# Attention and routed experts on one core: 512-column idle products, the fp16 identity made on GpSimd, and a new hand-written issue order

## The chip, the cores and the metric

One core of one Trainium2 chip. The time is that of the device, in microseconds (us), for one execution of the whole program; less is better. Engines: PE is TensorE (products), PEld its weight loads, DVE is VectorE, ACT ScalarE, POOL GpSimd, SP the engine that issues most transfers. Each engine takes its own instructions in order.

## What is computed

```python
# attention, per batch and head
q_s = exp(q - max(q, -1));  q_s /= sum(q_s, -1) + 1e-9
k_s = exp(k - max(k, seq)); k_s /= sum(k_s, seq) + 1e-9
kv  = einsum('bhsd,bhse->bhde', k_s, v)
x   = einsum('bhsd,bhde->bhse', q_s, kv)      # -> rows of 512, B*S = 8*576 rows
# routing, row after row within a batch
fresh_e = argmax(x @ w_gate)                   # 8 experts
e = fresh_e if s == 0 or sigmoid(x @ w_local) < 0.5 else prev_e
out = softmax(x @ w_gate)[e] * (relu(x @ w1[e]) @ w2[e])   # 512 -> 1024 -> 512
```

## The kernel before

The 4608 rows are four tiles t of 1152 (two batches each). Rows of one expert are gathered into blocks of 128. The first nine blocks, all of one expert, are drawn from tiles 0 and 1 alone, so that their products can run while tiles 2 and 3 are still in attention; after them come the blocks of the other experts, some 29 more.

The work up to block 8 is some 770 named tasks. Each has an engine, and `SWAP` lists the tasks that go to their second choice of engine. `ORDER` is one long list of the names; `emit` walks it and each engine gets its tasks in that sequence. No scheduler changes it afterwards. Names that matter here (a number behind a name is the batch, tile or block):

- `Lk Lv Lq`: loads of k, v, q (SP). `max kT kr ka kc sub exp`: the column maximum of k (DVE), its turn on PE, its spread (PE), a copy (ACT), the subtraction (DVE or POOL) and the exponential (ACT). `vc`: a copy of v. `mul`: the product of k and v, two halves a batch, 144 PE instructions each. `nsum norm turn hi lo KW put`: its normalization, and the gate's share of it.
- `qm qs qT qe`: the same for q. `xm xc inv xs ex gs`: a row group's product, its copy, and its store, and the gate's logits of a group.
- `g.* g1 .. g4 ra rp rb ac ab`: the routing of a pair of tiles, a chain of small DVE operations with short PE products between; `ro` makes one of 18 one-hot matrices (DVE, or two operations on ACT); `am` is the product that finds each block's rows; `ax` their indices.
- `G Gp`: gathers of a block's rows and shares (POOL); `Px Ph Pl` scale them and split them into two fp16 parts; `T`/`Tc` or `D` turn them; `W Wh Wl`: load and split of the first expert's weights; `F1 F2`: the block's two products, in halves of 96 and 24 instructions; `Ar Al` the ReLU and its fp16 rest; `Gv Pt`: scale the result (ACT) and scatter it (POOL).
- `RN.9`: ACT (high part) and DVE (rest) overwrite w1 with the second expert's; `s1 s2` load it in fp32. Block 9's code is written behind the list.
- `I`: an idle task, products of the identity that nobody reads:

```python
    def idle_mul(_):
        for i in range(8):
            nc.tensor.matmul(pd[:, 0:P], id16, id16, start=True, stop=True)
```

The `y` result has two buffers, so `Gv` of block 8 waits until the scatter `Pt` of block 6 has landed. The two turned maxima of k (`pz`) share one tile: an operation that reads one half waits for the last writer ahead of it in the list.

Of the kernel before, what the change touches and what calls it, by code (L numbers as in the profile page):

```python
# [116 lines left out]
Lk.0.0 I.72 Lk.0.1 max.0.0 max.0.1 kT.0 Lk.1.0 max.1.0 c2.1 Lq.0.0 Lk.1.1 kr.0 I.8 Lv.0.0 qm.0.0 ka.0 Lk.2.0 Lv.0.1 Lk.2.1 max.1.1 kc.0 qs.0.0 Lk.3.0  # L117
sub.0.0 vc.0.0 qs.0.1 exp.0.0 I.79 I.83 sub.0.1 qT.0.0 I.4 max.2.0 kT.1 I.15 kr.1 max.2.1 c2.0 qe.0.0 I.54 qT.0.1 ka.1 Lv.1.0 Lv.1.1 mul.0.0 vc.0.1
exp.0.1 qs.0.2 kc.1 vc.1.0 mul.0.1 max.3.0 I.78 qe.0.1 kT.2 sub.1.0 I.44 exp.1.0 Lk.3.1 cs sub.1.1 I.18 nsum.0 kr.2 I.20 ka.2 norm.0 Lk.4.0 vc.1.1
exp.1.1 I.13 Lv.2.0 qT.0.2 I.28 kc.2 Lv.2.1 max.3.1 Lq.0.1 mul.1.0 c2.2 mul.1.1 sub.2.1 sub.2.0 turn.0 qe.0.2 kT.3 vc.2.0 max.4.0 I.35 hi.0 kr.3  # L120
nsum.1 exp.2.0 Lk.4.1 I.29 norm.1 lo.0 exp.2.1 vc.2.1 ka.3 turn.1 mul.2.0 mul.2.1 Lk.5.0 sub.3.0 kc.3 hi.1 lo.1 qm.0.1 sub.3.1 exp.3.0 Lv.3.0 KW.0
nsum.2 norm.2 max.4.1 KW.1 put.0 put.1 xm.0.0 xm.0.1 xc.0.0 xc.0.1 qs.0.3 qs.0.4 qT.0.3 Lv.3.1 turn.2 qe.0.3 hi.2 qs.0.5 xm.0.2 qT.0.4 xc.0.2 qm.0.2
qe.0.4 xm.0.3 vc.3.0 lo.2 kT.4 xc.0.3 vc.3.1 kr.4 inv.0.0 Lk.5.1 xm.0.4 mul.3.0 exp.3.1 mul.3.1 KW.2 max.5.0 Lq.1.0 xc.0.4 Lv.4.0 qT.0.5 put.2 qs.0.6
nsum.3 qT.0.6 xs.0.0 norm.3 qe.0.5 qs.0.7 xm.0.5 qe.0.6 ex.0.0 qT.0.7 ka.4 xc.0.5 qe.0.7 max.5.1 turn.3 hi.3 inv.0.1 xm.0.6 qs.0.8 xc.0.6 qm.1.0
qs.1.0 lo.3 qT.0.8 gs.0.0 qm.1.1 ex.0.1 qe.0.8 kT.5 qm.1.2 qs.1.1 xm.0.7 KW.3 Lq.2.0 qs.1.2 qT.1.0 vc.4.0 put.3 xc.0.7 gs.0.1 qT.1.1 kr.5 qe.1.0
qe.1.1 kc.4 qs.1.3 xm.0.8 qT.1.2 xc.0.8 qe.1.2 xm.1.0 qT.1.3 xm.1.1 xc.1.0 qe.1.3 qs.1.4 xc.1.1 inv.0.2 qs.1.5 Lk.6.0 sub.4.0 xm.1.2 ex.0.2 xs.0.1
qT.1.4 qe.1.4 ka.5 xc.1.2 qT.1.5 exp.4.0 qs.1.6 qm.2.0 inv.1.0 xm.1.3 xm.1.4 gs.0.2 max.6.0 qe.1.5 qs.1.7 xc.1.3 xc.1.4 qT.1.6 qe.1.6 qT.1.7 qe.1.7
xm.1.5 sub.5.0 xc.1.5 qs.1.8 xs.0.2 ex.1.0 xm.1.6 qT.1.8 inv.1.1 xc.1.6 xm.1.7 qe.1.8 xc.1.7 xm.1.8 Lv.4.1 Lq.2.1 kc.5 I.21 qs.2.0 sub.4.1 xc.1.8
ex.1.1 Lv.5.0 gs.1.1 gs.1.0 exp.4.1 inv.1.2 mul.4.0 Lv.5.1 qT.2.0 ex.1.2 vc.4.1 qm.2.1 vc.5.0 gs.1.2 qe.2.0 mul.4.1 Lk.6.1 I.45 g.0.p0 qs.2.1 exp.5.0
g.0.p1 g.0 qT.2.1 nsum.4 Lv.6.0 g1.0 xs.1.2 qe.2.1 norm.4 g2.0 turn.4 mul.5.0 sub.5.1 g3.0 Lv.6.1 max.6.1 kT.6 g4.0 hi.4 vc.5.1 ra.0 I.1 exp.5.1 rp.0  # L130
vc.6.0 xs.1.1 lo.4 kr.6 I.24 vc.6.1 rb.0.p0 rb.0 ka.6 kc.6 Lk.7.0 mul.5.1 ro.0.4 Lk.7.1 ac.p0 nsum.5 I.43 I.68 W.0 ro.0.5 sub.6.0 ac ab norm.5 I.25
ro.1.7 ro.0.1 ro.0.3 I.39 ro.1.6 Lv.7.0 ro.1.2 W.1 qs.2.2 ro.1.0 I.53 KW.4 turn.5 ro.1.1 I.88 exp.6.0 ro.0.6 I.36 ro.1.5 ro.0.7 xs.1.0 ro.0.0 qs.2.3
ro.1.3 oe hi.5 Lq.2.2 mul.6.0 Wh.0 sub.6.1 exp.6.1 ro.0.2 put.4 I.48 mul.6.1 lo.5 max.7.0 Wl.0 ro.1.8 qs.2.4 KW.5 ro.0.8 I.33 nsum.6 ro.1.4 put.5
norm.6 qT.2.2 qe.2.2 am I.87 max.7.1 ax.p0 vc.7.0 xm.2.0 xc.2.0 Lv.7.1 kT.7 Wh.1 xm.2.1 ax.p1 xc.2.1 ax kr.7 W.2 G.0 ka.7 qT.2.3 kc.7 xm.2.2 qm.2.2
qT.2.4 sub.7.0 qs.2.5 qe.2.3 I.2 xc.2.2 sub.7.1 turn.6 qs.2.6 Wl.1 exp.7.0 Px.0 vc.7.1 of mul.7.0 inv.2.0 exp.7.1 mul.7.1 Lq.3.0 hi.6 qe.2.4 Ph.0 G.1
W.3 W.4 Wh.2 lo.6 nsum.7 KW.6 norm.7 qT.2.5 xs.2.0 xm.2.3 Pl.0 qs.2.7 put.6 T.0 qe.2.5 qT.2.6 Wl.2 xc.2.3 qm.3.0 Tc.0 Wh.3 xm.2.4 Wh.4 G.2 Sa.0 Px.1
F1.0.0 W.5 qe.2.6 Sb.0 Ar.0.0 turn.7 G.3 xc.2.4 Ph.1 Wl.3 hi.7 G.4 Wl.4 Al.0.0 Wh.5 qs.2.8 lo.7 Pl.1 F1.0.1 KW.7 Wl.5 Ar.0.1 qT.2.7 qs.3.0 W.6 qs.3.1
# [1112 lines left out]
```

## Time and profile before

| | us |
|---|---|
| median of 3 runs (lowest, highest) | 567.36 (566.24, 568.11) |
| the profiled execution, its own time | 568.54 |
| its span, first to last instruction | 566.8 |
| PE busy (share of the span) | 506.1 (89%) |
| DVE, ACT, POOL busy | 284.4, 221.1, 245.1 |
| profiled instructions | 18611 |

1.7 us of the profiled execution lie around the span. From about 128 us on PE is nearly always busy, so there what counts is PE's work and its few gaps; ahead of that PE mostly waits for others.

### The profile page before, as it was taken

The numbers are of one execution on the slowest core, as the hardware profiler recorded it, in microseconds if no ns is written. First come the engines' busy times: TensorE is split into PE (matmuls) and PEld (weight loads), VectorE is DVE, ScalarE is ACT, GpSimd is POOL, SyncE is SP. The second block draws the span as 40 slices with busy tenths as digits, with TensorE's granted clock in tenths as the row PEclk, the third lists the DMA queues.
The fourth block names the chain that finished last, engine by engine and source line by source line (L and its number), as shares of the span: only waits on it lengthen the run. The fifth ranks groups of instructions, "written<-read, shape, count | busy, mean of one in ns | idle before, by whom it ended". The sixth has DMA issues, their size and how long they took to land. (4 is left out here: it accounts for less than half of the span.)

```text
span 566.8 us, 18611 instructions
## 1 busy us (share of the span) xinstructions
PE 506.1 (89%) x7538; PEld 377.1 (67%) x7538; DVE 284.4 (50%) x487; ACT 221.1 (39%) x382; POOL 245.1 (43%) x260
## 2 busy tenths in 40 slices
...
GB/s 313 376 303 270 184 248 337 225 273 296 222 162 84 144 82 157 244 166 117 243 73 112 221 230 90 131 281 122 62 245 216 93 98 62 93 88 63 97 86 52
DMA packets 81541, 98.63 MB, mean 174 GB/s; under 512 B 46719, under 2 KB 56959, under 8 KB 81408
## 3 DMA queue, kind: packets, MB, share of 16 engines
...
q8 instruction: 83, 1.36, 1.1%
...
## 5 line engine op out<-in xcount | busy, mean ns | idle before, releaser
L900 PE MATMUL ph<-xT,w1h 128*128 128x128 f16 (+1 forms) x2432 | 180.3, 218 | 0.0
L900 PEld LDWEIGHTS <-w1h 128*128 128x128 f16 x2432 | 144.8, 98 | 0.0
L903 PE MATMUL ph<-xT,w1l 128*128 128x128 f16 (+1 forms) x1216 | 115.8, 218 | 9.2 <-DVEq L984 6.8
L912 DVE SCALAR_TENSOR_TENSOR lo<-ph,hi 128x512 f16<-128x512 f32 x76 | 52.3, 688 | 129.8 <-ACTq L984 114.2
L930 POOL DMA_INDIRECT out<-y,sidx x38 | 39.1, 1029 | 176.6 <-ACTq L984 140.8
L908 ACT ACTIVATE hi<-ph 128x512 f16<-128x512 f32 x76 | 45.2, 595 | 167.9 <-PE ph L900 115.4
L903 PEld LDWEIGHTS <-w1l 128*128 128x128 f16 x1216 | 82.0, 98 | 25.8 <-DVEq L984 7.0
L923 PEld LDWEIGHTS <-hi 128*128 128x128 f16 x608 | 56.3, 98 | 54.8 <-issue 1.1
L923 PE MATMUL py<-w2h,lo 128*128 128x512 f16 x184 | 69.8, 379 | 1.9 <-DVE lo L912 1.9
L923 PE MATMUL py<-w2h,hi 128*128 128x512 f16 x184 | 69.8, 379 | 0.0
L923 PE MATMUL py<-w2l,hi 128*128 128x512 f16 x184 | 69.7, 379 | 0.0
L863 DVE SCALAR_TENSOR_TENSOR x<-xn,x 128x512 f16<-128x512 f32 x37 | 30.1, 814 | 69.1 <-ACT x L188 65.1
L840 POOL DMA_INDIRECT xg<-xrows,gidx x42 | 47.1, 1122 | 35.0 <-DVE gidx L715 16.7
L923 PEld LDWEIGHTS <-lo 128*128 128x128 f16 x304 | 29.8, 98 | 38.9 <-DVE lo L912 2.9
L846 POOL DMA_INDIRECT pb<-shares,gidx x39 | 40.9, 1050 | 15.0 <-issue 6.0
L923 PE MATMUL pi<-w2h,hi 128*128 128x512 f16 x120 | 46.1, 384 | 0.0
L923 PE MATMUL pi<-w2l,hi 128*128 128x512 f16 x120 | 46.0, 383 | 0.0
L923 PE MATMUL pi<-w2h,lo 128*128 128x512 f16 x120 | 46.0, 383 | 0.0
L851 POOL TENSOR_TENSOR xn<-xg 128x512 f32<-128x512 f32 x34 | 36.3, 1068 | 11.6 <-DMA xg<-xrows,gidx 9.4
L926 ACT ACTIVATE y<-py,pb 128x512 f32<-128x512 f32 x23 | 15.8, 688 | 43.2 <-PE py L923 26.5
L350 PE MATMUL pd<-id 128*128 128x128 f16 x240 | 19.8, 240 | 11.4 <-DVE id L166 11.1
L353 DVE TENSOR_REDUCE KM<-KT 128x128 f32<-128x1152 f32 x13 | 28.2, 2182 | 3.5 <-DMA KT<-in_k 3.5
...
## 6 DMA issues: line engine op xcount, KB each, us to landing
...
```

The source lines that it names most:

```text
L350: nc.tensor.matmul(pd[:, 0:P], id16, id16, start=True, stop=True)
L353: nc.vector.tensor_reduce(out=KM[b % 2][:, 2 * u:2 * u + 2], in_=of(home("k", b, u), b, u).rearrange("p g c d -> p g d c"), axis=AX.X, op= ...
L840: nc.gpsimd.indirect_dma_start(out=xg[b % AHEAD], out_offset=None, in_=src, in_offset=bass.IndirectOffsetOnAxis(ap=i_[:, j_:j_ + 1], axis=0))
L846: nc.gpsimd.indirect_dma_start(out=pb[b % NPB], out_offset=None, in_=src, in_offset=bass.IndirectOffsetOnAxis(ap=i_[:, j_:j_ + 1], axis=0))
L851: eng.tensor_tensor(out=xn[b % 2].rearrange("p (g x d) -> p g x d", g=4, x=2), in0=xg[b % AHEAD].rearrange("p (g x) -> p g x", g=4)[:, :, ...
L863: nc.vector.scalar_tensor_tensor(out=x2[b % 2][:, 1, :], in0=xn[b % 2], scalar=XS, in1=x2[b % 2][:, 0, :], op0=ALU.mult, op1=ALU.subtract)
L900: nc.tensor.matmul(ph_[:, f, 0:n], W["w1h"][:, c, fs], xT_[:, i, c, 0:n], start=False, stop=(c == 3 and i == 1))
L903: nc.tensor.matmul(ph_[:, f, 0:n], W["w1l"][:, c, fs], xT_[:, 0, c, 0:n], start=(c == 0), stop=False)
L908: nc.scalar.activation(hi[b % 2][:, 4 * g:4 * g + 4, :], phs[g], AF.Relu)
L912: nc.vector.scalar_tensor_tensor(out=lo[b % 2][:, gs_, :], in0=phs[g], scalar=0.0, in1=hi[b % 2][:, gs_, :], op0=ALU.max, op1=ALU.subtract)
L923: nc.tensor.matmul(result(b), h_[:, f, :], w_[:, f, :], start=(f == 0 and i == 0), stop=(f == 7 and i == 2))
L930: nc.gpsimd.indirect_dma_start(out=outr, out_offset=bass.IndirectOffsetOnAxis(ap=i_[:, j_:j_ + 1], axis=0), in_=ys[b % 2], in_offset=None, ...
```

## The change

Three edits. An idle task issues two products of 512 columns in place of eight of 128 (four PE instructions for sixteen). The fp16 identity is cast by POOL, not DVE. `SWAP` and `ORDER` are replaced; there are 29 idle tasks where there were 30. All line numbers behind the tables grow by one.

```diff
 SWAP = """
-vc.0.0 norm.0 put.0 vc.1.1 put.1 vc.2.1 put.2 vc.3.0 vc.3.1 put.3 sub.4.1 norm.4 put.4 norm.5 put.5 norm.6 put.6 vc.7.0 vc.7.1 sub.7.1 put.7 gs.0.0
...
+vc.1.1 norm.1 put.1 vc.2.0 vc.2.1 norm.2 put.2 vc.3.0 vc.3.1 put.3 sub.4.1 norm.4 put.4 norm.5 put.5 vc.6.1 put.6 vc.7.0 vc.7.1 sub.7.1 norm.7 ex.0.0
...
 ORDER = """
-Lk.0.0 I.72 Lk.0.1 max.0.0 max.0.1 kT.0 Lk.1.0 max.1.0 c2.1 Lq.0.0 Lk.1.1 kr.0 I.8 Lv.0.0 qm.0.0 ka.0 Lk.2.0 Lv.0.1 Lk.2.1 max.1.1 kc.0 qs.0.0 Lk.3.0
...
+Lk.0.0 Lk.0.1 Lv.0.0 Lk.1.0 max.0.0 Lk.1.1 max.0.1 c2.1 I.65 kT.0 max.1.0 Lq.0.0 kr.0 ka.0 Lv.0.1 max.1.1 kc.0 qm.0.0 Lk.2.0 vc.0.0 Lv.1.0 c2.0
...
     id16 = cp.tile([P, P], F16, name="id16")
-    nc.vector.tensor_copy(out=id16, in_=ident)
+    nc.gpsimd.tensor_copy(out=id16, in_=ident)
...
     def idle_mul(_):
-        for i in range(8):
-            nc.tensor.matmul(pd[:, 0:P], id16, id16, start=True, stop=True)
+        for i in range(2):
+            nc.tensor.matmul(pd, id16, id16.unsqueeze(1).to_broadcast([P, 4, P]), start=True, stop=True)
```

**First place: PE, the first k-v products.** Before, `mul.0` (the two rows of 36) stands behind seven idle tasks and is followed by another; `pz` rows are `kT` and `ka`.

```order
L470 MATMUL pq<-ident,qs 128x128 x4
L368 MATMUL pz<-ident,mt 64x128 x4
L403 MATMUL pa<-VP_123,KT_115 64x65 x36
L403 MATMUL pa<-VP_124,KT_116 64x65 x36
L350 LDWEIGHTS id_67
L350 MATMUL pd<-id_67 128x128
```

After, on PE at the same place:

```order
L404 MATMUL pa<-VP_123,KT_115 64x65 x36
L404 MATMUL pa<-VP_124,KT_116 64x65 x36
L359 MATMUL pz<-ident,KM_126 128x128 x2
L369 MATMUL pz<-ident,mt 64x128 x4
L432 MATMUL pq<-ident,R_134 128x128 x2
L404 MATMUL pa<-VP_125,KT_117 64x65 x36
L471 MATMUL pq<-ident,qs 128x128 x4
```

Three idle tasks of four instructions stand ahead of these, and none between `mul.0` and `mul.1` (the third row of 36).

**Second place: DVE, the routing of tiles 0 and 1.** Before, from `g2` (the scan into `cs`) to `rb` (the first `pf` with `pq`); the row into `KM` is `max.6.1`.

```order
L572 SCALAR_TENSOR_TENSOR cs<-pq,va 1x256
L353 TENSOR_REDUCE KM_126<-KT_115 128x128
L583 TENSOR_TENSOR E<-pq,nA 128x18
L584 TENSOR_TENSOR E<-E,sc 128x18
L586 TENSOR_TENSOR OH<-E,iota_em 128x72 x2
L619 SCALAR_TENSOR_TENSOR pf<-cj,OH 128x144
L621 CAST cc<-pf 128x16
L438 SCALAR_TENSOR_TENSOR kvT<-pq,kvT 128x256
L362 TENSOR_REDUCE mt<-pz 128x4
L633 TENSOR_TENSOR pf<-pf,pq 128x144
```

After, on DVE:

```order
L573 SCALAR_TENSOR_TENSOR cs<-pq,va 1x256
L584 TENSOR_TENSOR E<-pq,nA 128x18
L585 TENSOR_TENSOR E<-E,sc 128x18
L587 TENSOR_TENSOR OH<-E,iota_em 128x72 x2
L620 SCALAR_TENSOR_TENSOR pf<-cj,OH 128x144
L622 CAST cc<-pf 128x16
L354 TENSOR_REDUCE KM_126<-KT_115 128x128
L634 TENSOR_TENSOR pf<-pf,pq 128x144
```

`max.6.1` has moved behind `ra`, where DVE waits for PE's `rp` anyway, and `lo.4` and `kr.6` have left the chain.

**Third place: the hand-over to the second expert, on DVE and POOL.** Before, DVE from `RN.9.0` (w1l) to `RN.9.1`; the row into `x` is `Pl.9`, the rows into `cB` and `info` the last piece of `bj`, the row into `lo` is `Al.8.0`.

```order
L946 SCALAR_TENSOR_TENSOR w1l<-s_3429,w1h 128x4x128 x4
L984 UNCONDITIONAL_BRANCH x2
L863 SCALAR_TENSOR_TENSOR x_1842<-xn_1840,x_1842 128x512
L789 TENSOR_REDUCE cB<-g2B 1x43
L790 TENSOR_TENSOR info_78<-cB,erB 1x43
L791 TENSOR_SCALAR info_78<-wB 1x43
L792 CAST info_78<-wB 1x43
L912 SCALAR_TENSOR_TENSOR lo_1853<-ph_2147,hi_1851 128x512
L984 COMPARE_AND_BRANCH
L946 SCALAR_TENSOR_TENSOR w1l<-s_3429,w1h 128x4x128 x4
```

After, on DVE (the row into `xn` is `Px.11`):

```order
L947 SCALAR_TENSOR_TENSOR w1l<-s_2915,w1h 128x4x128 x4
L985 UNCONDITIONAL_BRANCH x2
L852 TENSOR_TENSOR xn_1719<-xg_1717 128x512
L718 TENSOR_SCALAR tz_3839<-tk_3838 128x43
L719 SCALAR_TENSOR_TENSOR sidx_77<-tk_3838,tz_3839 128x43
L985 COMPARE_AND_BRANCH
L947 SCALAR_TENSOR_TENSOR w1l<-s_2915,w1h 128x4x128 x4
L985 UNCONDITIONAL_BRANCH x2
L913 SCALAR_TENSOR_TENSOR lo_1732<-ph_1981,hi_1730 128x512
```

`Al.8.0`, for which PE's `F2.8.0` waits, now stands behind `RN.9.1`; `bj` has left this stretch. On POOL before, from `Pt.5` to `Pt.6` (the rows into `out` are `Pt.5`, `Pt.7`, `Pt.6`; the row into `xg` is `G.12`, and `L860`/`L861` are `Pl.11`):

```order
L930 DMA out<-y_1856,sidx_73 4608x512
L984 UNCONDITIONAL_BRANCH
L930 DMA out<-y_1856,sidx_73 4608x512
L846 DMA pb_1848<-shares,gidx_76 128x1
L851 TENSOR_TENSOR xn_1840<-xg_1838 128x512
L984 UNCONDITIONAL_BRANCH
L860 TENSOR_SCALAR xn_1840<-xn_1840 128x512
L861 TENSOR_TENSOR x_1842<-xn_1840,x_1842 128x512
L840 DMA xg_1835<-xrows,gidx_76 128x592
L886 UNCONDITIONAL_BRANCH
L930 DMA out<-y_1855,sidx_73 4608x512
```

After, on POOL (`Pt.5`, `Px.10`, `G.12`, `Pt.6`, then `Pt.7` and `Pl.11`):

```order
L931 DMA out<-y_1735,sidx_73 4608x512
L852 TENSOR_TENSOR xn_1718<-xg_1716 128x512
L841 DMA xg_1714<-xrows,gidx_76 128x592
L931 DMA out<-y_1734,sidx_73 4608x512
L985 UNCONDITIONAL_BRANCH
L931 DMA out<-y_1735,sidx_73 4608x512
L985 UNCONDITIONAL_BRANCH
L861 TENSOR_SCALAR xn_1719<-xn_1719 128x512
L862 TENSOR_TENSOR x_1721<-xn_1719,x_1721 128x512
```

`Pt.6` now stands ahead of `Pt.7` and `Pl.11`. Elsewhere: `F1.0.0` now has 14 `mul`, 23 `qT` and 22 `xm` ahead of it on PE, where it had 16, 25 and 23; the same work stands behind it.

## Rows read from the trace of the kernel before

**Rows 1.** Busy time (count) by engine in the hand-over; granted clock, DMA share, GB/s

```profile
core 0: us, PE busy (x) PEld busy (x) DVE busy (x) ACT busy (x) POOL busy (x), PEclk, DMA share, GB/s
241.40:274.50 33.10, 22.25 (x204) 14.69 (x202) 17.20 (x27) 8.85 (x17) 15.52 (x14) 0.90 0.69 147
```

**Rows 2.** The page's DMA queues: packets, MB, share of 16 engines

```profile
q8 instruction: 83, 1.36, 1.1%
```

**Rows 3.** The same windows view, cut where PE stood still twice

```profile
0.00:27.05 27.05, 9.93 (x222) 8.59 (x223) 18.82 (x21) 7.31 (x10) 13.97 (x37) 1.00 0.97 343
27.05:45.08 18.03, 13.16 (x381) 11.84 (x381) 12.23 (x15) 8.82 (x15) 10.09 (x11) 0.89 0.93 322
```

**Rows 4.** PE in order of time: start, us, what [idle before <-releaser]

```profile
27.06 0.34 PE L403 MATMUL pa<-VP,KT 64*64 64x65 f32 x6 [3.62 <-issue]
...
33.10 2.33 PE L403 MATMUL pa<-VP,KT 64*64 64x65 f32 x144
...
45.09 0.48 PE L403 MATMUL pa<-VP,KX 64*64 64x65 f32 x5 [4.32 <-issue]
```

**Rows 5.** DVE in order of time, early

```profile
28.76 1.36 DVE L384 TENSOR_TENSOR KT<-KT,pz 128x1152 f32<-128x1152 f32 x1 [3.97 <-PE pz L358]
```

**Rows 6.** DVE in order of time, first and second routing

```profile
82.51 1.70 DVE L456 TENSOR_REDUCE qm<-qt 128x24 f32<-128x1536 f32 x1
...
84.92 2.06 DVE L543 SCALAR_TENSOR_TENSOR fl<-L,st 128x18 f32<-128x18 f32 x1
...
97.79 2.53 DVE L639 TENSOR_SCALAR lb<-lb 128x18 f32<-128x18 f32 x1
...
195.59 0.40 DVE L543 SCALAR_TENSOR_TENSOR fl<-L,st 128x18 f32<-128x18 f32 x1
...
209.01 0.28 DVE L639 TENSOR_SCALAR lb<-lb 128x18 f32<-128x18 f32 x1
```

**Rows 7.** POOL in order of time, first routing

```profile
84.30 2.63 POOL L384 TENSOR_TENSOR KT<-KT,kb 128x1152 f32<-128x1152 f32 x1
...
97.66 2.63 POOL L384 TENSOR_TENSOR KT<-KT,kb 128x1152 f32<-128x1152 f32 x1 [8.62 <-ACT kb L378]
```

**Rows 8.** ACT in order of time, the first of the one-hot matrices

```profile
100.56 0.40 ACT L650 ACTIVATE da<-iot,off 128x128 f32<-128x128 f16 x1 [2.98 <-DVE off L640]
101.00 0.49 ACT L651 ACTIVATE oo<-da,val,nval 128x128 f16<-128x128 f32 x1
```

**Rows 9.** PE in order of time: `am`, and the start of `F1.0.0`

```profile
112.06 0.60 PE L704 MATMUL pq<-oba,oo 128*128 128x9 f16 x18 [1.13 <-ACT R L188]
...
127.89 0.38 PE L903 MATMUL ph<-xT,w1l 128*128 128x128 f16 x4
```

**Rows 10.** PE in order of time: one `xm`, one `qT`

```profile
66.19 0.75 PE L483 MATMUL pa<-R,qe 64*64 64x74 f32 x32
...
67.17 0.65 PE L470 MATMUL pq<-ident,qs 128*128 128x128 f32 x4
```

**Rows 11.** PE in order of time: five idle tasks; a 512-column product

```profile
99.60 2.41 PE L350 MATMUL pd<-id 128*128 128x128 f16 x40
...
136.70 0.38 PE L923 MATMUL py<-w2h,hi 128*128 128x512 f16 x1
```

**Rows 12.** PE in order of time, hand-over

```profile
245.29 0.39 PE L923 MATMUL py<-w2h,lo 128*128 128x512 f16 x1 [1.90 <-DVE lo L912]
...
248.89 0.38 PE L903 MATMUL ph<-xT,w1l 128*128 128x128 f16 x4 [1.27 <-DVE xT L190]
...
268.03 0.61 PE L903 MATMUL ph<-xT,w1l 128*128 128x128 f16 x4 [6.82 <-DVEq L984]
```

**Rows 13.** ACT in order of time, hand-over

```profile
240.44 2.18 ACT L188 ACTIVATE w1h<-s 128x512 f16<-128x512 f32 x4
...
265.39 0.69 ACT L926 ACTIVATE y<-py,pb 128x512 f32<-128x512 f32 x1 [10.95 <-DMA out<-y,sidx]
```

**Rows 14.** POOL in order of time, hand-over

```profile
253.48 1.10 POOL L930 DMA_INDIRECT out<-y,sidx  x1 [0.30 <-issue]
```

**Rows 15.** DVE in order of time, hand-over

```profile
245.16 2.48 DVE L946 SCALAR_TENSOR_TENSOR w1l<-s,w1h 128x512 f16<-128x512 f32 x4
```

72 lines of the change are left out of this document (36 added, 36 removed).

## The prediction

> **What bounds the kernel now.** I read the page first, and from it that the kernel has two parts. Up to the first product of block 0 (`F1.0.0`, which starts at 127.89 [rows 9]) PE mostly waits for others; behind it PE is nearly always busy, and a microsecond counts only if it removes PE work or one of PE's few gaps. So I cut PE's timeline at its waits, and asked of each what was late.
>
> Two early waits have no releaser: "issue", 3.62 us inside `mul.0.1` at 27.06 and 4.32 us at `mul.2.1` at 45.09 [rows 4]. No engine and no load ends them. Their place tells more: 222 + 223 PE instructions stand ahead of the first, and 381 + 381 = 762 between the two, close to 3 x 256 [rows 3]. The page's queue of instructions brought 83 packets of 1.36 MB together, 16.4 KB each [rows 2]; 18611 instructions over 83 packets are 224 each on average. I read the stalls as PE having come to the end of what had been fetched, every 256 of its instructions, while the next packet was behind loads: the DMA share is 0.97 and 0.93 there [rows 3]. A stretch full of `mul` is worst, since its 144 instructions a half last 2.33 / 2 = 1.17 us (144 products, and as many weight loads, take 2.33 for two halves [rows 4]). DVE's first `sub` (at 28.76) then waited 3.97 us for `pz` [rows 5], whose last writer, `kT`, stood on PE behind the stalled product: a stall of PE became a late start of everybody.
>
> Next comes the routing of tiles 0 and 1, a chain on DVE from which `am`, the gather and `F1.0.0` follow. I looked at its smallest operations, since nothing there should take a microsecond, and compared the second routing: the operation of L543 took 2.06 against 0.40 and that of L639 2.53 against 0.28 [rows 6]. Each began within 0.7 us of a POOL subtraction of 2.63 [rows 7]: DVE was stretched while POOL worked. Ahead of them stands a `qm` of 1.70 that the routing doesn't need [rows 6].
>
> In the steady part I looked for gaps of PE above 1 us. Most lie at the hand-over from the first expert's blocks to the others: of 33.10 us PE is busy 22.25 at a granted clock of 0.90 [rows 1]. Three waits carry it, 1.90 for `Al.8.0`, 1.27 for block 9's turn, and 6.82 before block 10 [rows 12], together 10.0. The last is a queue: `Gv.8` on ACT waited 10.95 us for the scatter `Pt.6` [rows 13], issued by POOL only at 253.48 [rows 14] and landed at 265.39, 11.9 us later. Everything of ACT behind it, block 10's work too, was late by this.
>
> **The change part by part.** *Stalls.* An idle task now issues 4 instructions for 16. Ahead of `mul.0` stand three tasks where seven stood, so 12 for 112. The first stall stands at about 445 instructions [rows 3]; the same count (449 by the program, with unrecorded ones) falls, along the new order, in the middle of `mul.1.0`, the one before it near the end of `mul.0.0`. Between them stand turns that wait for DVE and a `mul` that waits for another batch's loads, time for a fetch. I take the first stall off with 0.2 left: -3.4 (bounds 0, and -4.0 by `sub`'s wait [rows 5]). The second boundary after that (961) falls again in `mul.2.1`, its line full of `mul` as before: 0 for the second stall (to -4.3).
>
> *The routing.* In the new order `qm` no longer stands ahead of L543, `max.6.1` is behind `ra` where DVE waits anyway, and `lo.4` and `kr.6` are gone from the chain. What can be won is 2.06 - 0.40 = 1.66, 2.53 - 0.28 = 2.25, and 1.70; `max.6.1` is bounded by another pass over the same 128x1152, 1.36 [rows 5]. The sum of 7.0 is one end, 0 the other (POOL still has subtractions to do, and may meet the chain elsewhere). I take -4: about the two stretched operations, or one of them and the two passes.
>
> *One-hot matrices.* From the first on ACT (100.56 [rows 8]) to `am` (112.06 [rows 9]) are 11.5 us, in which ACT made 7 of 18 and did much else. In the new order nine stand there with nearly nothing between; a pair takes 0.40 + 0.49 and some 0.04 between [rows 8], 9 x 0.93 = 8.4. That would be -3.1; I take -2 since DVE makes the other nine beside its own work (bounds 0 and -3.1).
>
> So `F1.0.0` moves from 127.89 by -9.4 to 118.5. *Moved work.* That isn't all won: PE has 14 `mul`, 23 `qT` and 22 `xm` ahead of it for 16, 25 and 23, and does the rest later, when it is the bound: 2 x 1.17 [rows 4] + 2 x 0.65 + 0.75 [rows 10] = 4.4, +4.3 with some of it in gaps.
>
> *Hand-over.* `Pt.6` is issued ahead of `Pt.7` and `Pl.11` now, so `Gv.8` should find `y` free and the wait of 6.82 go. Against this, `Al.8.0` stands behind `RN.9.1` on DVE, four operations of 2.48 together [rows 15], and ahead of both stands `Px.11`, which waits for a gather issued later than before. What waits behind `Al.8.0` is `F2.8.0` on PE. I guess an idle of some 6.5 there in place of 10.0: -3.5. Bounds: -6.8, when only the two small waits stay or move, and +7, when the scatter's 11.9 us delay [rows 13, 14] recurs for a gather: 17 in all.
>
> *At nothing.* Five idle tasks take 2.41 us, 0.48 each; a product of 512 columns takes 0.38 per row [rows 11], two 0.76. That is at most 0.28 more for each of 29, where PE waits for loads or DVE; uncovered, it would be 8.1 us. POOL's cast of the identity lets the first turn start earlier, but `mul.0` waits for v and the maxima; PE's start is not moved. If POOL's cast were late instead, idle products would slip, not the loads.
>
> **Sum**, against the profiled execution's 568.54: -3.4 - 4 - 2 + 4.3 - 3.5 = -8.6, so 559.9. The median of the runs is 1.2 lower, so 558.8 on its scale; I say 559.5.
>
> **The rivals.** *The second stall goes too.* Fewer idle instructions and a shifted start may give the fetch time. For it: the packet's transfer competes with loads, and these end earlier if the first stall goes. Against: the line that ends there is still packed with `mul`. It gives 4.3 more, about 555.
>
> *The stalls have another cause.* If what follows were resident long ahead, PE would not have run out at a boundary, the stall would belong to `mul` itself or to its transfer of operands, and come again at the new place: 3.4 lost, 562.9. The 762 instructions between the stalls [rows 3] speak against it, two stalls alone are few.
>
> [...]
>
> *The change doesn't reach the end of the front.* The loads keep the DMA at 0.97 and 0.93 [rows 3]; if the data set the pace, a stall won is lost again at the next load, the routing starts when its last tile is there, and `F1.0.0` moves by about 1 us. Then the hand-over's gain and the moved work cancel, 568.3: no change. Against it: DVE's 3.97 us for `pz` [rows 5] were no load's.
>
> *Slower: the hand-over's queue on DVE.* `Px.9`, `Pl.9`, `RN.9.0`, `Px.11`, `RN.9.1`, `Al.8.0` now stand in this sequence on DVE. If block 11's gather lands as late as `Pt.6` did, 11.9 us from its issue [rows 13, 14], `RN.9.1` and `Al.8.0` wait for it, and PE has neither `F2.8.0` nor block 9. The front's net is -9.4 + 4.3 = -5.1, so the whole is slower by over 0.3% when the hand-over idles for more than 10.0 + 5.1 + 1.7 = 16.8 us. With 17 idle and a front that gives 2 us less it is 570.5. For it: all three links are in the new order; against it: those gathers are issued behind few others.
>
> **How the numbers follow.** Forecast 0.48; the second stall too 0.17; another cause 0.08; the front is held 0.13; slower 0.14. The likeliest's own range is 556 to 563 (routing 0 to -7 and hand-over within 3 of my guess, seldom both at one end). For the whole, 551 takes in the second stall with the routing's or hand-over's better end, 570 the held front and part of the slower case. A measurement of this kernel tells about 0.3%, 1.7 us, from no change: faster is below 565.7, slower above 569.1. The first three cases are faster (0.73, less what their bad ends take: 0.70), the held front is the same (0.14), the rest slower (0.16).
>
> **What would show it.** Right: no wait of more than 1 us with "issue" in `mul.0`, the first `sub` on DVE without 3.97 us for `pz`, L543 and L639 below 0.5, `am` near 102.7 and `F1.0.0` near 118.5, `Gv.8` without a wait for a scatter, and one gap of 5 to 8 us for `lo` before `F2.8.0`. A stall of 3 to 4 us still at `mul.2.1` is part of the forecast. Wrong: a stall at `mul.1.0` in place of `mul.0.1` (the fetch is still late), L543 or another small operation again stretched beside POOL, `am` on time but `F1.0.0` held by the gather or by `T.0`, or a gap above 10 us before `F2.8.0`. Largest in doubt are the routing's -4 and the hand-over's -3.5, which is a guess between ends 14 us apart.

## The result and the profile after

The change makes the kernel faster by about 1%: the ratio to before is 0.988, with a 95% interval of 0.984 to 0.992. That ratio leaves out the long executions of either kernel; the medians of all 20 are only 0.4% apart (567.05, from 557.79 to 573.89, against 569.38, from 564.34 to 575.24). A wait that the change brought, shown below, makes some of its executions long; in how many of them it stands isn't known. The profiled execution took 565.09 against 568.54.

Its page, the lines on the span and on the engines:

```profile
span 563.3 us, 18254 instructions
...
PE 512.0 (91%) x7356; PEld 369.7 (66%) x7356; DVE 278.0 (49%) x482; ACT 224.0 (40%) x390; POOL 249.7 (44%) x265
```

The windows, with the columns of [rows 1]: the hand-over, and the two stretches of [rows 3].

```profile
241.00:274.50 33.50, 32.34 (x333) 22.51 (x334) 13.85 (x20) 11.17 (x20) 16.93 (x16) 0.90 0.96 209
0.00:27.05 27.05, 13.57 (x180) 8.58 (x180) 18.40 (x23) 7.77 (x10) 9.45 (x35) 1.00 0.97 351
27.05:45.08 18.03, 13.37 (x328) 9.73 (x330) 12.49 (x14) 7.37 (x14) 12.86 (x13) 0.72 0.96 327
```

PE is busy for 32.34 us of the hand-over with 333 products, where it was 22.25 of 33.10 with 204 [rows 1]; the stretch is one of time, so it doesn't hold the same work. In the second stretch of the front the granted clock is lower than it was (0.72 for 0.89 [rows 3]). PE in order of time tells what became of the waits:

```profile
20.39 4.18 PE L404 MATMUL pa<-VP,KT 64*64 64x65 f32 x144 [0.75 <-ACT KT L389]
...
28.38 1.73 PE L404 MATMUL pa<-VP,KT 64*64 64x65 f32 x72
...
44.42 0.58 PE L404 MATMUL pa<-VP,KX 64*64 64x65 f32 x23 [1.01 <-issue]
...
59.69 0.38 PE L484 MATMUL px<-R,qe 64*64 64x74 f32 x1 [2.51 <-issue]
...
76.76 1.11 PE L471 MATMUL pq<-ident,qs 128*128 128x128 f32 x4 [1.85 <-POOL qs L462]
...
83.41 0.75 PE L484 MATMUL pa<-R,qe 64*64 64x74 f32 x32
...
105.73 0.20 PE L705 MATMUL pq<-oba,oo 128*128 128x9 f16 x2
...
120.95 0.38 PE L904 MATMUL ph<-xT,w1l 128*128 128x128 f16 x4
...
139.63 0.38 PE L904 MATMUL ph<-xT,w1l 128*128 128x128 f16 x4 [2.35 <-DMA xT<-x]
...
238.39 0.38 PE L924 MATMUL py<-w2l,hi 128*128 128x512 f16 x1
242.16 0.61 PE L924 MATMUL py<-w2h,lo 128*128 128x512 f16 x1 [3.38 <-DVE lo L913]
242.55 0.63 PE L924 MATMUL py<-w2h,hi 128*128 128x512 f16 x1
242.98 0.63 PE L924 MATMUL py<-w2l,hi 128*128 128x512 f16 x1
...
432.60 1.04 PE L901 MATMUL ph<-xT,w1h 128*128 128x128 f16 x8 [4.65 <-issue]
```

The stall of 3.62 in `mul.0.1` [rows 4] is gone: the two halves of `mul.0` run through, though in 4.18 us, where two halves took 2.33 [rows 4], and `mul.1` starts at 28.38 for 33.10. The one at `mul.2.1` is 1.01 for 4.32 [rows 4], and another of 2.51 stands in tile 0's `xm`. That one isn't new: before had one of 2.54 in `xm`, which [rows 4] leaves out.

```profile
61.29 0.49 PE L483 MATMUL pa<-R,qe 64*64 64x74 f32 x16 [2.54 <-issue]
...
79.51 0.75 PE L483 MATMUL pa<-R,qe 64*64 64x74 f32 x32
```

The second row is the end of tile 1 before, `xm.1.8`; it answers to 83.41 after. `am` (its first products at 105.73) and `F1.0.0` at 120.95 are 6.3 and 6.9 us earlier than in [rows 9]. In the hand-over one wait is left, 3.38 for `lo`; behind it a 512-column product takes 0.43 from start to start (242.55 to 242.98), where it took 0.21 (238.18, the product ahead of the rows shown, to 238.39): the granted clock is 0.51 from 242.16 to 247.60 (0.50 from 242.50 to 243.50), and 1.00 from 247.60 to 250.00. And at 432.60, deep in the blocks, a wait "issue" of 4.65 us is new.

The 4.18 us of `mul.0` are near half rate too: 29 ns for each of its 144 products, where those of before took 16 (2.33 us). The windows view's 1.00 doesn't tell it, since the trace's first record of the granted clock starts at 25.6 (before: at 13.9). It comes and goes: `mul.0` took 4.05 to 4.18 in seven of the ten traces of the new order and 2.33 in three, the second trace of the change among them.

```profile
20.75 2.33 PE L404 MATMUL pa<-VP,KT 64*64 64x65 f32 x144 [0.75 <-ACT KT L389]
```

Two of the seven have the old idle tasks, so the new form of the idle products isn't what does it; what else in the order does is open.

DVE, ACT and POOL, the rows that answer to [rows 5 to 8] and [rows 13, 14]:

```profile
25.22 1.35 DVE L385 TENSOR_TENSOR KT<-KT,pz 128x1152 f32<-128x1152 f32 x1 [1.86 <-PE pz L359]
...
71.49 1.97 DVE L462 TENSOR_TENSOR qs<-qa,qm 128x512 f32<-128x512 f32 x1
...
86.70 0.17 DVE L544 SCALAR_TENSOR_TENSOR fl<-L,st 128x18 f32<-128x18 f32 x1
...
97.08 0.18 DVE L640 TENSOR_SCALAR lb<-lb 128x18 f32<-128x18 f32 x1
```

```profile
97.51 0.40 ACT L651 ACTIVATE da<-iot,off 128x128 f32<-128x128 f16 x1 [2.74 <-DVE off L641]
...
252.68 0.69 ACT L927 ACTIVATE y<-py,pb 128x512 f32<-128x512 f32 x1 [0.21 <-DMA pb<-shares,gidx]
```

```profile
70.26 2.64 POOL L385 TENSOR_TENSOR KT<-KT,kb 128x1152 f32<-128x1152 f32 x1 [1.43 <-ACT kb L379]
...
238.08 1.50 POOL L931 DMA_INDIRECT out<-y,sidx  x1 [0.91 <-issue]
```

The two routing operations take 0.17 and 0.18 us, where [rows 6] have 2.06 and 2.53, and `Gv.8` waits 0.21, not 10.95 [rows 13].

To compare runs I cut each profiled execution at the first products of five tasks on PE's timeline. Behind block 9 the code of all kernels is the same. `F2.9.1` is the first group of second products (`F2`) behind the wait of 6.82 [rows 12], `F2.37.1` the last group of all.

| run | to F1.0.0 | to F2.8.0 | to F2.9.1 | to F2.20.0 | to F2.37.1 |
|---|---|---|---|---|---|
| before | 127.89 | 114.90 | 27.78 | 109.45 | 177.19 |
| the change | 120.95 | 117.23 | 21.95 | 108.70 | 184.43 |
| difference | -6.94 | +2.33 | -5.83 | -0.75 | +7.24 |

### The profile page after: what moved, and what is told of

The parts are those of the page before. It is cut to its first block, busy times and chain, and to the rows that moved or that the text cites. A ratio compares the mean times of both kernels' runs of the same rounds, so it can differ in the third digit from the quotient of the medians.

```text
span 563.3 us, 18254 instructions
## 1 busy us (share of the span) xinstructions
PE 512.0 (91%) x7356; PEld 369.7 (66%) x7356; DVE 278.0 (49%) x482; ACT 224.0 (40%) x390; POOL 249.7 (44%) x265
## 3 DMA queue, kind: packets, MB, share of 16 engines
q8 instruction: 82, 1.34, 1.1%
## 5 line engine op out<-in xcount | busy, mean ns | idle before, releaser
L924 PE MATMUL py<-w2h,lo 128*128 128x512 f16 x184 | 71.2, 387 | 3.4 <-DVE lo L913 3.4
L924 PE MATMUL py<-w2h,hi 128*128 128x512 f16 x184 | 71.1, 387 | 0.0
L924 PE MATMUL py<-w2l,hi 128*128 128x512 f16 x184 | 71.0, 386 | 0.0
L841 POOL DMA_INDIRECT xg<-xrows,gidx x42 | 45.1, 1075 | 17.3 <-issue 11.3
L847 POOL DMA_INDIRECT pb<-shares,gidx x39 | 42.2, 1083 | 14.7 <-DMA shares<-pr 7.3
L189 ACT ACTIVATE x<-xn 128x512 f16<-128x512 f32 x39 | 24.3, 628 | 17.7 <-ACTq L985 10.2
```

Source lines behind the costliest of these rows:

```text
L189: nc.scalar.copy(out, in_) if scale is None else nc.scalar.activation(out, in_, AF.Copy, scale=scale)
L841: nc.gpsimd.indirect_dma_start(out=xg[b % AHEAD], out_offset=None, in_=src, in_offset=bass.IndirectOffsetOnAxis(ap=i_[:, j_:j_ + 1], axis=0))
L847: nc.gpsimd.indirect_dma_start(out=pb[b % NPB], out_offset=None, in_=src, in_offset=bass.IndirectOffsetOnAxis(ap=i_[:, j_:j_ + 1], axis=0))
L924: nc.tensor.matmul(result(b), h_[:, f, :], w_[:, f, :], start=(f == 0 and i == 0), stop=(f == 7 and i == 2))
```

## The experiments

**Is the early stall the end of 256 instructions?** The order of before, with two products of 512 columns in an idle task; and the order of the change, with eight of 128. A line, here and in the prediction, is the 256 PE instructions from one such end to the next.

```diff
-        for i in range(8):
-            nc.tensor.matmul(pd[:, 0:P], id16, id16, start=True, stop=True)
+        for i in range(2):
+            nc.tensor.matmul(pd, id16, id16.unsqueeze(1).to_broadcast([P, 4, P]), start=True, stop=True)
```

> The order of before with the two 512-column idle products of after. Theory (the early stalls are PE reaching the end of its fetched instructions, every 256 of them): with 12 fewer instructions per idle task the counts fall elsewhere; the line that is nearly all product of k and v, and so is run through in about 2.2 us, now ends at 93% of mul.1.1. So no stall in mul.0.1 and none at mul.2.1, but one of 2 to 4 us in mul.1.1. F1.0.0 stays within 3 us of 127.89, the wait of 6.82 at the hand-over stays, the time is within 0.5% of before. Rival 1 (the stalls belong to the products themselves): waits of 3 to 4 us stay at mul.0.1 and mul.2.1. Rival 2 (the idle products carry the gain of the change): F1.0.0 near 121 and 4 to 7 us faster than before.

> The change with the eight 128-column idle products of before. Theory (fetch every 256 instructions): the lines that end at 93% of mul.1.1 and at 93% of mul.3.1 are run through fastest, so stalls of 2 to 4 us there and none at mul.2.1; the front is set by other waits (POOL's subtraction ahead of the q work of tile 1), so F1.0.0 stays at 120 to 123, and the hand-over is that of after: 1.5 to 2% faster than before when no late stall falls into the run, within 0.4% of after. Rival (the idle products carry the gain): F1.0.0 back near 127, no faster than before by more than the hand-over's 8 us less 5.

PE's products of k and v in the old order with the new idle task, and then PE's waits in the new order with the old one:

```profile
21.18 2.33 PE L403 MATMUL pa<-VP,KT 64*64 64x65 f32 x144
...
28.76 2.25 PE L403 MATMUL pa<-VP,KT 64*64 64x65 f32 x137
34.76 0.34 PE L403 MATMUL pa<-VP,KT 64*64 64x65 f32 x7 [3.74 <-issue]
...
43.39 1.56 PE L403 MATMUL pa<-VP,KX 64*64 64x65 f32 x43 [2.71 <-issue]
```

```profile
35.08 0.34 PE L404 MATMUL pa<-VP,KT 64*64 64x65 f32 x7 [2.32 <-issue]
...
64.07 0.59 PE L404 MATMUL pa<-VP,KX 64*64 64x65 f32 x10 [3.32 <-issue]
```

The stall left `mul.0.1` and came to `mul.1.1`, 137 products into `mul.1`, 7 before its end (3.74); in the other kernel it came to `mul.1.1` (2.32) and `mul.3.1` (3.32), as expected. One in the middle of `mul.2.1` (2.71) I hadn't expected, and the other kernel has 1.34 there and 2.57 in `xm`. So these waits follow the count of instructions, not the work. The count shows it best: in all fourteen traces every "issue" wait above 0.8 us ahead of `F1.0.0` comes 222 + 127 n PE products from the start, n a whole number, within 4 products; 127 products and their weight loads are 254 instructions, close to 256. With the semaphore instructions that the trace has on PE, 768, 769, 1023 and 512 stand from each to the next of the five of before, within 1 of 3, 3, 4 and 2 times 256. And the waits are fetches: in 72 of the 73 above 0.9 us, all along the traces, a packet of 16 KB on the queue of instructions landed 1.1 to 1.7 us before the wait's end (2.2 in the last one).

Fewer instructions win nothing in the old order: 1.000 (0.995 to 1.006), `F1.0.0` at 134.22 for an expected 125 to 131, with a wait of 3.31 on the fetch right ahead of it. In the trace of the new order with the old idle task the gain at `F1.0.0` is gone: it comes at 129.09, where I expected 120 to 123, which is the rival's sign. The ratio is 0.9925 (0.989 to 0.996), short of the 1.5 to 2% that I expected. So the smaller count is worth something in the new order, though not in the old. Ahead of `F1.0.0` the waits on the fetch above 0.8 us add up to 12.6 to 14.4 us in the old order, to 10.7 and 11.4 in the new order with the old idle tasks, and to 3.5 to 8.2 with the new ones.

**Is the hand-over's gain the place of `Pt.6`?** One name moved in each order.

In the old order:

```diff
-Gv.7 Pt.7 Al.8.0
+Gv.7 Pt.6 Pt.7 Al.8.0
...
-G.12 D.11 Pt.6 Al.8.1
+G.12 D.11 Al.8.1
```

In the change:

```diff
-Ph.11 Pt.6 Ar.8.1 s1.9 Al.8.0 Pt.7 Tc.9 Pl.11 Pl.10 Al.8.1
+Ph.11 Ar.8.1 s1.9 Al.8.0 Pt.7 Tc.9 Pl.11 Pl.10 Pt.6 Al.8.1
```

> The order of before with one name moved: the scatter Pt.6 stands ahead of Pt.7 on POOL. Theory (the hand-over's 6.82 us hang on when Pt.6 is issued): Gv.8 no longer waits 11 us, the wait of 6.82 in block 10 goes, front unchanged (F1.0.0 at 127 to 129), F2.20.0 some 6 to 8 us earlier than 380.0, the time 1.0 to 1.4% shorter. Rival (block 10 is held by its gather, its turn or its weights, which Pt.6 only hides): a wait of 4 us or more stays ahead of block 10 with another releaser, and the time is within 0.5% of before.

> The change with Pt.6 put back behind Pt.7, Pl.11, D.10 and D.11 of the order. Theory: the wait of Gv.8 for the scatter returns with 6 to 11 us and block 10 waits for it, 5 to 8 us more than after; the front is that of after (F1.0.0 at 120 to 122), F2.20.0 at 373 to 377 where after had 368.8, so still 0.5 to 1.2% faster than before. Rival (the hand-over's gain comes from the other moves: bj gone from DVE, Gp.9 and G.12 elsewhere): F2.20.0 within 2 us of 368.8.

The old order with `Pt.6` moved: POOL and ACT in order of time, and the hand-over's window.

```profile
238.97 1.53 POOL L930 DMA_INDIRECT out<-y,sidx  x1 [7.54 <-ACT hi L908]
...
252.02 0.69 ACT L926 ACTIVATE y<-py,pb 128x512 f32<-128x512 f32 x1 [0.57 <-PE py L923]
```

```profile
241.00:274.50 33.50, 30.64 (x330) 21.04 (x329) 16.36 (x28) 11.30 (x21) 20.80 (x17) 1.00 0.75 215
```

In the old order the first theory holds: `Gv.8` no longer waits for the scatter, the stretch to `F2.9.1` falls from 27.78 to 19.10, and the ratio is 0.990 (0.986 to 0.993; median 561.16 against 569.07). One name gives as much as the whole change. In the new order it failed: with `Pt.6` put back the stretch is 21.76 for 21.95, the ratio 0.991 (0.9865 to 0.996). ACT's row and two of POOL's of that run say why; the last one here is POOL's of before:

```profile
260.18 0.69 ACT L927 ACTIVATE y<-py,pb 128x512 f32<-128x512 f32 x1 [0.59 <-DMA out<-y,sidx]
```

```profile
248.84 1.79 POOL L861 TENSOR_SCALAR xn<-xn 128x512 f32<-128x512 f32 x1 [1.47 <-ACT x L189]
...
252.25 1.04 POOL L931 DMA_INDIRECT out<-y,sidx  x1 [0.16 <-issue]
```

```profile
249.26 1.49 POOL L860 TENSOR_SCALAR xn<-xn 128x512 f32<-128x512 f32 x1 [4.88 <-DVE x L192]
```

Three things took 10.4 of the 10.95 us, counted from the start of `F2.8.0` (245.68 here, 242.79 before). `Pt.6` was issued 6.6 us behind it, not 10.7 [rows 14]: `Pl.11` ahead of it waited 1.47 for `Ph.11`, now on ACT, where it had waited 4.88 for DVE, and `G.12` no longer stands between the two. The scatter landed 7.9 us from its issue, not 11.9. And ACT came to `Gv.8` 13.9 us behind the start, not 11.7. So the place of `Pt.6` is enough in the old order; in the new one the other moves take the wait away without it.

**What is left of the hand-over's loss, and of the front's?** Two moves of one name in the change: `Al.8.0` right behind `Ar.8.0`, and `sub.5.1` behind `qs.1.8`.

```diff
-RN.9.0 Ar.8.0 Pt.5
+RN.9.0 Ar.8.0 Al.8.0 Pt.5
...
-s1.9 Al.8.0 Pt.7
+s1.9 Pt.7
```

> The change with one name moved: Al.8.0 stands right behind Ar.8.0, ahead of Px.11 and RN.9.1 on DVE. Theory (what is left of the hand-over's loss is F2.8.0 waiting for Al.8.0, and a lower granted clock behind that wait): the wait of 3.4 to 4.2 us for lo falls below 1, the stretch from F2.8.0 to F2.9.1 (21.8 to 23.0 in the runs with the new order) falls to 17 to 19, and the time is 3 to 5 us below that of the change (medians 564 to 567), so 561 to 563. Rival (DVE's queue is late as a whole and the wait moves to block 9's turn or to w1l): the stretch stays above 21 and the time is that of the change.

```diff
-vc.5.0 sub.5.1 sub.5.0
+vc.5.0 sub.5.0
...
-inv.1.0 qs.1.8 Lv.6.0
+inv.1.0 qs.1.8 sub.5.1 Lv.6.0
```

> The change with one name moved: sub.5.1, the subtraction of 2.6 us on POOL, stands behind qs.1.8 instead of ahead of qs.1.6. Theory (in the new order this subtraction holds the q work of tile 1, which moves xm.1.8 from 79.5 to 83.4 and eats the gain of the stall that was removed): PE's wait of 1.85 for qs near 77 goes, xm.1.8 comes 2 to 3.5 us earlier than in the runs of the new order (83.4 and 85.3), am and F1.0.0 by as much. In the time: 0 to 3 us, since PE has work to do anyway behind F1.0.0. Rival (tile 1's q work is held by the loads or by PE): xm.1.8 at 83 to 86 as in the change.

PE's waits of the first in the hand-over; then, of the second, two rows of DVE and one each of POOL and PE:

```profile
241.44 0.39 PE L924 MATMUL py<-w2h,lo 128*128 128x512 f16 x1 [0.45 <-DVE lo L913]
245.44 0.38 PE L904 MATMUL ph<-xT,w1l 128*128 128x128 f16 x4 [1.67 <-DVE xT L191]
257.62 0.38 PE L904 MATMUL ph<-xT,w1l 128*128 128x128 f16 x4 [1.48 <-DMA xT<-x]
```

```profile
70.50 0.68 DVE L462 TENSOR_TENSOR qs<-qa,qm 128x512 f32<-128x512 f32 x1
...
77.73 1.92 DVE L505 TENSOR_SCALAR xt<-xt 128x24 f32<-128x24 f32 x1
```

```profile
76.94 2.66 POOL L385 TENSOR_TENSOR KT<-KT,kb 128x1152 f32<-128x1152 f32 x1
```

```profile
79.66 0.75 PE L484 MATMUL pa<-R,qe 64*64 64x74 f32 x32
```

`Al.8.0` first: the wait of 3.38 is 0.45, but 1.67 for the turn and 1.48 for block 10's transposition take part of its place; 19.90 to `F2.9.1`, short of the 17 to 19 expected. The ratio of 0.972 (0.966 to 0.979) is the lowest of all, but over few executions with 549 to 570 between them; 2 us of it are accounted for, the rest isn't. `sub.5.1` later: `xm.1.8` at 79.66 for 83.41. In this run `mul.0` took 2.33, so the second run of the change, below, with 2.33 too and `xm.1.8` at 81.99, is the fairer one to compare: 2.3 us, as expected. But the way is another than I wrote: POOL's queue held nothing. While POOL subtracted (70.26 to 72.90), DVE's `qs.1.5` took 1.97 us; with the subtraction elsewhere it takes 0.68, and the maximum that the q work waits for follows it. The subtraction now falls beside another small operation of DVE, which took 0.18 in the change (at 80.00) and 1.92 here; it ends at 79.65, POOL's subtraction at 79.60. `F2.8.0` starts at 235.96; the ratio is 0.988 (0.982 to 0.993).

**The quiet routing alone**, in the old order with `Pt.6` moved.

```diff
-xc.1.3 xc.1.4
+xc.1.3 kc.5 xc.1.4
...
-qs.1.8 xs.0.2
+qs.1.8 sub.5.1 xs.0.2
...
-Lq.2.1 kc.5 I.21
+Lq.2.1 I.21
...
-mul.5.0 sub.5.1 g3.0 Lv.6.1 max.6.1 kT.6 g4.0
+mul.5.0 g3.0 Lv.6.1 g4.0
...
-rp.0 vc.6.0 xs.1.1 lo.4 kr.6 I.24 vc.6.1 rb.0.p0 rb.0 ka.6
+rp.0 max.6.1 kT.6 vc.6.0 xs.1.1 I.24 vc.6.1 rb.0.p0 rb.0 lo.4 kr.6 ka.6
```

> The order of before with Pt.6 ahead of Pt.7 (ratio 0.990 alone) and, of the change's front, the quiet routing chain alone: sub.5.1 behind qs.1.8 on POOL (kc.5 ahead of it), max.6.1 and kT.6 behind rp.0, kr.6 and lo.4 behind rb.0. Theory (small DVE operations are stretched while POOL subtracts): the operations of L543 and L639 take below 0.5 us where they took 2.06 and 2.53, rb.0 at 91 to 93 instead of 97.5, am and F1.0.0 3 to 5 us earlier than 112 and 128 to 129, F2.3.0 1 to 4 us earlier than 180 to 181, the time 1 to 4 us below that of the move of Pt.6 alone (561.2). Rival 1 (the stretch isn't POOL's): L543 or L639 still above 1 us. Rival 2 (an earlier F1.0.0 wins nothing, since the rest of the attention must be done anyway): F2.3.0 at 180 or later, and the time within 1 us of 561.2.

DVE, then ACT and PE, in order of time:

```profile
86.00 0.49 DVE L543 SCALAR_TENSOR_TENSOR fl<-L,st 128x18 f32<-128x18 f32 x1
...
97.86 0.18 DVE L639 TENSOR_SCALAR lb<-lb 128x18 f32<-128x18 f32 x1
```

```profile
100.13 0.27 ACT L378 COPY kb<-pz 128x128 f32<-128x128 f32 x1 [2.70 <-PE pz L368]
100.29 0.40 ACT L650 ACTIVATE da<-iot,off 128x128 f32<-128x128 f16 x1
```

```profile
111.81 0.79 PE L403 MATMUL px<-VP,KT 64*64 64x65 f32 x34 [2.53 <-issue]
...
114.55 0.67 PE L704 MATMUL pq<-oba,oo 128*128 128x9 f16 x18
```

The stretch was POOL's: both operations are short once no subtraction runs beside them. But `am` is at 114.55, later than 112.06 [rows 9], and `F1.0.0` at 129.97. The one-hot matrices of ACT stand behind `kc.6`, which now waits for a later `kT.6`; the first starts at 100.29, hardly earlier than at 100.56 [rows 8]. So the shorter chain won nothing, since ACT wasn't free behind it. The rest of the delay is PE's: a fetch of 2.53 now falls into the `mul` ahead of `am`. The time is 560.04, that of `Pt.6` alone (561.16, on another chip) within what can be told, as in the second rival.

**The cast on DVE**, in the change, and the change once more.

```diff
-    nc.gpsimd.tensor_copy(out=id16, in_=ident)
+    nc.vector.tensor_copy(out=id16, in_=ident)
```

> The change with the fp16 identity cast by DVE as before. Theory (the cast is worth nothing): the first idle product starts at 11 instead of 2.3, kT.0 at about 12 instead of 6.9, but mul.0.0 within 1 us of 20.4 to 21.1 and the time that of the change within 0.4%. It is also a second look at how far the front scatters: F1.0.0 in 121 to 129. Rival (the early turn counts): mul.0.0 and all behind it 3 us or more later.

> The change itself, unaltered, run beside the three below on the same chip, for their comparison and for the scatter of its front and of the late stall. If the gain over before is the hand-over's alone: F1.0.0 anywhere in 121 to 127, the stretch from F1.0.0 to F1.8.0 108 to 112 (103 to 106 in the old order), from F2.8.0 to F2.9.1 21.5 to 23 (27.8 before), and a ratio to before of 0.985 to 0.995. If the front carries it: F1.8.0 at 230 or earlier.

With the cast on DVE `mul.0` starts at 20.78 and the ratio is 0.985 (0.979 to 0.9905), no worse than the change: no gain from POOL's cast can be seen. The change again has 0.987 (0.9815 to 0.992), and `F1.0.0` at 119.33, earlier than expected. `F1.8.0` comes at 227.90 (229.50 in the first trace of the change), ahead of 230, which I had named as the sign that the front carries the gain; but `Al.8.0` first and `Pt.6` late, with the same order ahead of it, have it at 231.85 and 236.97 (before: 233.28).

**Both moves together**, with either idle task, and with `Tc.9` ahead of `RN.9.1`.

```diff
-Gv.7 Sd.1 bx RN.9.1 Ph.10
+Gv.7 Sd.1 bx Tc.9 RN.9.1 Ph.10
...
-Pt.7 Tc.9 Pl.11
+Pt.7 Pl.11
```

> The change with Al.8.0 right behind Ar.8.0 (which alone gave a ratio of 0.972) and sub.5.1 behind qs.1.8. Theory: the two moves act at different places and add: F1.0.0 at 117 to 122, xm.1.8 at 79 to 82, F2.8.0 to F2.9.1 17 to 20; median 2 to 4 us below that of Al.8.0 alone and 6 to 10 us below the change, 553 to 558. Rival (an earlier front is lost to the attention work behind F1.0.0): F1.8.0 as in the change and the ratio again 0.972 or above.

> The same with the eight 128-column idle products, 348 more PE instructions ahead of block 9, so that every later end of 256 instructions falls 92 instructions elsewhere in the blocks' code. Theory (the late waits with the releaser issue, 3 to 5 us in block 12 to 30 of the runs with the new order, are fetches that happen to fall beside the transposes and gathers of a block): no late wait above 2 us, or at another block; early stalls at mul.1.1 and mul.3.1 instead, so F1.0.0 1 to 5 us later than in both_moves; the time within 0.5% of it. Rival (the late waits are random): they come or not in either.

> both_moves with Tc.9, the copy of block 9's turn, ahead of RN.9.1 on DVE. Theory: the wait of 1.67 us ahead of F1.9.0 for it (in the run of Al.8.0 alone) falls below 0.5, F2.8.0 to F2.9.1 1 to 1.5 us shorter than in both_moves; the time 0.1 to 0.3% less, too little to tell. Rival: RN.9.1 is 0.7 us later and F1.9.0 waits for w1l instead, no gain.

| run | median | lowest to highest | ratio | to F1.0.0 | to F2.8.0 | to F2.9.1 | to F2.20.0 | to F2.37.1 |
|---|---|---|---|---|---|---|---|---|
| old order, new idle | 571.98 | 564.02 to 581.63 | 1.000 | 134.22 | 112.28 | 24.91 | 109.79 | 176.65 |
| old order, Pt.6 first | 561.16 | 556.95 to 565.00 | 0.990 | 129.52 | 111.76 | 19.10 | 108.53 | 176.64 |
| the same, quiet routing | 560.04 | 557.80 to 563.08 | 0.985 | 129.97 | 114.24 | 19.08 | 108.76 | 176.70 |
| change, old idle | 564.45 | 560.68 to 568.93 | 0.9925 | 129.09 | 117.67 | 22.97 | 108.11 | 178.21 |
| change, Pt.6 late | 565.93 | 558.46 to 573.80 | 0.991 | 126.27 | 119.41 | 21.76 | 112.98 | 178.20 |
| change, Al.8.0 first | 556.25 | 549.14 to 569.77 | 0.972 | 121.45 | 118.95 | 19.90 | 110.31 | 184.78 |
| change, sub.5.1 later | 561.54 | 559.49 to 570.23 | 0.988 | 118.52 | 117.44 | 21.99 | 113.73 | 176.65 |
| change, cast on DVE | 561.56 | 556.39 to 570.80 | 0.985 | 124.02 | 120.71 | 21.27 | 109.80 | 176.65 |
| change again | 559.77 | 557.86 to 567.94 | 0.987 | 119.33 | 117.12 | 22.36 | 112.94 | 184.15 |
| both moves | 558.99 | 554.86 to 565.04 | 0.982 | 120.72 | 118.81 | 20.09 | 108.81 | 184.13 |
| both, old idle | 560.89 | 558.52 to 562.63 | 0.989 | 123.78 | 118.13 | 20.11 | 108.30 | 176.65 |
| both, turn first | 561.52 | 555.33 to 565.78 | 0.987 | 120.53 | 117.82 | 19.31 | 113.56 | 183.23 |

The moves didn't add up: both have a median of 558.99 for the 553 to 558 that I expected, and 0.982 (0.976 to 0.989) isn't clearly below the change's 0.987 on the same chip. With the old idle task `F1.0.0` is 3.1 us later than with the new one, as expected. `Tc.9` first shortened its stretch by 0.8 us, for the 1 to 1.5 expected, and the time can't tell. What the last column shows matters more. The same wait stands on PE in three of these runs and in the change:

```profile
436.10 1.03 PE L901 MATMUL ph<-xT,w1h 128*128 128x128 f16 x8 [4.86 <-issue]
```

```profile
434.75 1.03 PE L901 MATMUL ph<-xT,w1h 128*128 128x128 f16 x8 [4.72 <-issue]
```

```profile
432.24 1.03 PE L901 MATMUL ph<-xT,w1h 128*128 128x128 f16 x8 [4.65 <-issue]
```

These are the change again, `Al.8.0` first and both moves. In all of them, in the change and in the one with the turn first it falls on the 1376th product from the end of the program (1.4 there in the run with `Pt.6` late, put down to ACT), and one of 1.3 to 3.8 falls on the 2567th in five runs (0.5 in another); that one shows in the stretch to `F2.20.0`. Behind the first eight products take 1.03 for 0.61, the lower clock again (granted 0.59 from 432.60 to 440.00 in the change), so that 184.1 stands for 176.65. All eight runs with the new order and the new idle task have a wait at one of these two places. Neither place has one in the six runs with another count of instructions ahead of it. Both stand in the middle of a group, a few products behind others that read the same tiles, so it wasn't data that was missing. At the 1376th the packet of instructions took 1.0 to 1.1 us, like most, but started 1.9 to 2.4 us after PE had stopped; at the 2567th it took 2.1 to 3.6 in four of the five.

## Why the prediction was right, and where it wasn't

The forecast was 559.5 with 551 to 570; the time lies inside by its median (567.05) and by its ratio (0.988 of 567.36 is 560.6). That it does is in part luck. By the ratio the gain is 6.8 us, where 7.9 was forecast; by the medians of all 20 it is 2.3, and in the profiled execution 3.5. There the front won 4.6 and the hand-over 5.8, and a late wait that wasn't in the sum took 7.2 back: errors of both signs.

- **The stall at `mul.0.1`: the mechanism was right, its worth was not.** It went, by the count of instructions; the first subtraction of batch 1 came 3.5 us earlier (25.22 for 28.76 [rows 5]) and `mul.1.0` 4.7. But at the end of tile 1 (`xm.1.8`) the front was 3.9 us late (83.41, and 79.51 before), and at the routing's first small operation still 1.8 (86.70, and 84.92 [rows 6]): the term of -3.4 was lost before the routing began. Of what took it two parts are seen: `mul.0` at half rate (1.85 us) and `qs.1.5`, held beside the subtraction that the change had moved off the routing (1.3 of its own, 2.3 for the whole move by the experiment). The lower clock behind 27 us (0.72 for 0.89) is another, not priced. The step that failed is the one that carried the whole stall on to `F1.0.0`. The second stall fell to 1.01, where the sum took nothing off it.
- **"Two early waits"** was too few: before has five "issue" waits above 0.8 us ahead of `F1.0.0`, 13.2 us together, and the change two, 3.5 together. Nor was the transfer of the packet slow at the two that I read: it took 1.10 and 1.06, as most do, but started 1.1 and 2.0 us after PE had stopped. Whether loads held back its start is not shown.
- **The rival that the stalls belong to the products** fell: they moved with the count in both directions, and the stalls of 2 us and more came at new ends of 256 when it changed (`mul.1.1` 3.74 in the old order with the new idle task; `mul.1.1` 2.32 and `mul.3.1` 3.32 in the new order with the old one).
- **The routing, -4:** from the operation of L543 (L544 after) to ACT's first one-hot 15.64 became 10.81 (84.92 to 100.56 before [rows 6, 8], 86.70 to 97.51 after), -4.8. Right, and the cause as stated, with one thing more in the rows: the two long operations end 0.05 and 0.03 us behind POOL's subtraction [rows 6, 7]. They were held until it ended, rather than slowed.
- **The one-hot matrices, -2 (to -3.1):** from that one-hot to `am` 11.50 became 8.22, -3.3, a little past the bound. Right, and more needed than I saw, since without them the routing's gain doesn't reach `am` (the quiet routing alone).
- **Moved work, +4.3:** from `F1.0.0` to `F2.8.0` the change takes 2.33 more; over the eight runs of the new order with the new idle task 117.1 to 120.7 against 111.8 to 114.9 in the three of the old order with the old one. Right in size. A wait of 2.35 for block 1's transposition at 139.63 was not in the sum.
- **So the front** nets -4.6 at `F2.8.0` in the profiled execution (forecast -5.1), but it scatters: the change's own front (once with the cast on DVE), without the move of `sub.5.1`, starts `F2.8.0` at 236.5 to 245.7 in five runs, before's at 242.8 and 241.3. That the front gains at all is not shown; the rate of `mul.0` and the waits on the fetch differ from run to run of one code.
- **The hand-over, -3.5:** mis-sized. It gave -5.8 (27.78 to 21.95), since the waits there were 3.38 where I guessed 6.5. With `Al.8.0` early 2 us more are won.
- **At nothing:** POOL's cast was rightly put there. The idle products were not: no cost of their own can be seen, but 12 instructions fewer in each move every later end of 256, and in the change one of them falls where the fetch is late, 7 us in some executions. Why its packet starts late there isn't shown; that it falls beside a block's transfers was argued, and the packet itself took no longer than others. Six of the eight profiled executions of these kernels lie above their medians, so how often it happens can't be told from them.
- **A sum of the slower rival** is wrong: 17 us idle and a front that gives 2 us less make 568.54 + 7.0 - 3.1 = 572.4. The 570.5 given there has the whole front in it.
